# Experts' rows turned by VectorE and regrouped through DRAM instead of transposed by TensorE

## Chip, cores and metric

The kernel runs on one core of a Trainium2 chip. The metric is the time of one execution on the device in microseconds (us); lower is better. Fast and slow differ here by fractions of a per cent: the three runs of the kernel before lie between 3649.78 and 3657.06 us.

## What is computed

Three layers, one after the other, on 8 sequences of 3072 tokens with 256 channels (24576 tokens), all in float32:

```python
def _attn_ref(x, filt_r, filt_i):            # a filter in the frequency domain
    Y = np.fft.rfft(x, axis=1) * (filt_r + 1j * filt_i)[None]
    return np.fft.irfft(Y, n=x.shape[1], axis=1)

def _moe_ref(x, w_gate, w_output_gate, w1, w2):   # 8 experts, each token to one
    e_idx = np.argmax(x @ w_gate, axis=1)
    for e in range(E):
        mask = e_idx == e
        h = np.maximum(x[mask] @ w1[e], 0.0)
        out[mask] = gate_w[mask, None] * eom[mask, e, None] * (h @ w2[e])

def _moe2_ref(x, w_in, w_out):               # a layer for all tokens
    h = x @ w_in
    return (h / (1.0 + np.exp(-1.702 * h))) @ w_out
```

## The kernel before

The program has three stages. The first (to about 540 us) filters the sequences by a Fourier transform in steps and leaves the rows of all tokens in DRAM (`yn`), and a table that lists each expert's tokens (`xid`). The second, about 540 to 1690 us, runs the experts. The third, to the end, runs the last layer and puts each row in its token's place. The change lies in the second stage alone.

**Blocks and slots.** `experts(js)` runs over a list `js` of blocks, one expert each: 41 full blocks of 512 rows and 17 halves of 256 (four more halves stand behind a branch that isn't taken here). The first 11 are full; from then on every third is a half. A block has eight slots (`f` from 0 to 7). In each slot TensorE runs `gemm1` of this slot (six matmuls, L590) and `gemm2` of the slot two before (six matmuls, L599). Every operand is split in a high and a low part, so that three products give float32 accuracy. ScalarE makes the high part `hh` with the rectifier (L912) and VectorE the low part `hl` (L913); `gemm2` two slots later uses both. In the same slot an eighth of the next block's weights is split (`split_w`, L654 on ScalarE, L655 on VectorE). While full blocks run, VectorE also converts the last layer's weights, a piece a slot (`convert`, L745 to L759), from about 700 to 1130 us.

**How rows come in.** For block `j` of the list, the next `ja` and the one after it `jb`:

- `load_tok(jb)` in slot 4 (POOL): an indirect DMA loads the tokens' numbers (`ids` L667, for halves `it` L688), then four indirect DMAs (two for a half) gather 128 rows of 256 each into `xg` (L693). Two buffers of `xg`.
- `scale_x(ja)` in slot 2 (POOL): the rows of `xg` are multiplied by their gate (L705).
- `prep_x(ja, k)` at the end of slots 4 and 5: `split_t` has TensorE transpose `xg` (L575, four for a full block, two for a half) into PSUM, and `split_out` makes `xh` (ScalarE, L580) and `xl` (VectorE, L581) from it.
- `load_w(jb, 0)` and `load_w(jb, 1)` in slots 3 and 7 (SP's queue): the weights, 1 MB each, into one buffer each (`w1r` L618, `w2r` L623). SP also stores a block's results (`zt`, L949) in slot 1 of the block after it.

Each engine runs its instructions in the order in which the program writes them and stands where one has to wait. POOL isn't bound to the slots as such: it runs ahead as far as buffers allow. Only while tokens are still being scattered into `xid` (`scatter`, L399 and L402, one each slot, in blocks 0 to 6) does each of its steps wait for a tick of that slot. `NE` is the number of first blocks that take tokens of the first four sequences alone, so that they needn't wait for the last scatters.

`turn_rows` in the third stage has VectorE turn 32x32 blocks (L1168, `V.transpose`), and lets 16 DMAs put these in place. The experts' stage doesn't use it before the change.

Of the kernel before, what the change touches and what calls it, by code (L numbers as in the profile page):

```python
# [24 lines left out]
NT = 32  # L25
CAP = NTOK
NFULL = 41
NE = 8
BE = 4
NX = 5  # L30
NU = 5
# [95 lines left out]
def fftconv_moe_moe2(ctx: ExitStack, tc: tile.TileContext, x, ffl, fny, wg, w1, w2, win, wout,  # L127
# [5 lines left out]
    yn = tc.dram_tile([NTOK, D], F32, name="yn")  # L133
    zt = tc.dram_tile([2, 128, NZ], F32, name="zt")
    idc = tc.dram_tile([NZ - ZREM, 1], I32, name="idc")
    us = [tc.dram_tile([N1, N2, D], F32, name=f"us{b}") for b in range(NB)]

    keep = ctx.enter_context(tc.tile_pool(name="keep", bufs=1))
# [436 lines left out]
            T.transpose(p[:, c, :], xg[:, c, 128 * k:128 * k + 128], eye)  # L575
        return p

    def split_out(p, nt, xh, xl, k):
        w = slice(0, 128 * nt)
        S.copy(xh[:, k, w], p[:, 0:nt, :].rearrange("p c t -> p (c t)"))  # L580
        V.tensor_tensor(xl[:, k, w], p[:, 0:nt, :].rearrange("p c t -> p (c t)"),  # L581
                        xh[:, k, w].bitcast(F32), op=ALU.subtract)

    def gemm1(wh, wl, xh, xl, f, w):
        p = pools["ph"].tile([128, 512], F32, name="ph", tag="ph")
# [86 lines left out]
    def load_tok(j):  # L672
        if j is None:
            return
        nt = nt_of(j)
        assert j < NE or not (scat or gating)
        if nt == 4:
            if j in named:
                G.memset(gap, 0.0)
            else:  # L680
                load_ids(j)
            it = ids[:, j]
        else:
            G.memset(gap, 0.0)
            it = pools["m"].tile([128, 2, 2], I32, name="it")
            for c in range(2):
                o = NFULL + 2 * (j - NFULL) + c
                G.indirect_dma_start(  # L688
                    out=it[:, c, :], out_offset=None, in_=xid,
                    in_offset=bass.IndirectOffsetOnAxis(ap=xidx[:, o:o + 1].bitcast(U32), axis=0))  # L690
        t = pools["m"].tile([128, 4, D], F32, name="xg")
        for c in range(nt):
            i = G.indirect_dma_start(  # L693
                out=t[:, c, :], out_offset=None, in_=yn if j >= NE else yn[0:BE * SEQ, :],
                in_offset=bass.IndirectOffsetOnAxis(ap=it[:, c, 0:1].bitcast(U32), axis=0))
            early(j, i)
        xg[j] = t, it
# [13 lines left out]

    rof = {}

    def prep_x(j, k):
        if j is None:
            return
        if k == 0:
            xt[j] = [pools["xt"].tile([128, 2, 512], F32R, name="xh"), pools["xt"].tile([128, 2, 512], F32R, name="xl")]
        p = split_t(xg[j], nt_of(j), k)
        split_out(p, nt_of(j), *xt[j], k)  # L720
        if k == 1:
            xg.pop(j)

    cv = {}

# [96 lines left out]
    for k in range(ng * NB + 4 + nu):  # L822
        b, i = divmod(k, ng)
        if k == kt:
            c1.close()
            c1p.close()
            open_expert_pools()
            load_tok(0)
        if k < kt:
            load_u(k + NU - 1)  # L830
            if k < 6:
                load_f(k + 2)
            prep_f(k + 2)
            if k == 8:
                nc.sync.dma_start(smt, t_sm)
            swap(k - 1)
            filt_a(k)
            filt_b(k - 1)
            inv2_out(k - 3)
            if k in s1_at:  # L840
                stage1(s1_at[k])
                stage1_out(s1_at[k])
            inv2(k - 2)
        if k in t2_at:
            trans(*t2_at[k])
        if k - 1 in t2_at:
            inv1(*t2_at[k - 1])
        if kt <= k < kt + 7:
            for m in PARTS[max(0, k - kt + 1 if k > kt else 0):k - kt + 2]:
                load_part(0, m)  # L850
        if kt + 4 < k < kt + 9:
            for m in PARTS[2 * (k - kt - 5):2 * (k - kt - 5) + 2]:
                split_w(0, m)
        if k == kt + 9:
            load_w(1, 0)
        if k == kt + 11:
            load_w(1, 1)
        if k == kt + 3:
            scale_x(0)
        if k == kt + 6:  # L860
            load_tok(1)
        if k in (kt + 9, kt + 10):
            prep_x(0, k - kt - 9)
        if k in (kt - 24, kt - 22):
            load_ids((k - kt + 24) // 2)
        if 3 <= k < kt:
            pb, pg = divmod(k - 3, ng)
            scatter(2, gts[pb % 2][:, 0, 0, 8 * pg:8 * pg + 1])
        elif k in t2_at:
            scatter(1, tick(gq[t2_at[k]][:, 0, 0:1]))  # L870
        go_on(2 if k < kt else 1)
        if i == 1 and b > 1:
            go_on(1000)
            gating.append(gate(b - 2, psa, "pt"))
            if b - 2 == BE - 1:
                gating.append(early_tables())
# [9 lines left out]
        nc.sync.dma_start(zg[j], zt[:, :, at].rearrange("k p n -> p k n"))  # L886

    first = {}

    def experts(js):  # L890
        ex = None
        hq, pz = {}, {}
        ns = 8 * len(js)
        js = js + [None, None]
        for t in range(ns + 2):
            if t == ns - 12 and not first:
                first["rest"] = nc.values_load(eidx[0:1, NBLK:NBLK + 1], min_val=0, max_val=NREM)
                tc.mark_branch_hint_location("rest", "LikelyTaken", [ET.PE, ET.DVE, ET.Activation])
            if t == ns - 8 and "hi" not in first:
                first["hi"] = pools["z0"].tile([128, 2, 512], F32R, name="z0h", bufs=1)  # L900
                for k in range(2):
                    z, h = zg[0][:, k, :], first["hi"][:, k, :]
                    S.copy(h, z)
                    V.tensor_tensor(z.bitcast(F32R), z, h.bitcast(F32), op=ALU.subtract)
            n, f = divmod(t, 8)
            j, ja, jb = (js + [None])[n:n + 3]
            if t < ns:
                w = 128 * nt_of(j)
                p = gemm1(wt[j][0], wt[j][1], *xt[j], f, w)
                hh = pools["m"].tile([128, 512], F32R, name="hh", bufs=3)  # L910
                hl = pools["m"].tile([128, 512], F32R, name="hl", bufs=3)
                S.activation(hh[:, 0:w], p[:, 0:w], AF.Relu)  # L912
                V.scalar_tensor_tensor(hl[:, 0:w], p[:, 0:w], 0.0, hh[:, 0:w].bitcast(F32),  # L913
                                       op0=ALU.max, op1=ALU.subtract)
                hq[t] = hh, hl
                split_w(ja, f)
                if f == 3:
                    load_w(jb, 0)
                if f == 7:
                    load_w(jb, 1)  # L920
                if f == 4:
                    load_tok(jb)
                scatter(1, tick(hh[:, 0:1].bitcast(F32)))
                go_on(1)
                if f == 2:
                    scale_x(ja)
                if not wm and not gating and not scat:
                    open_layer_pools()
                    S.activation(gap2, gap2, AF.Gelu_apprx_sigmoid)
                    ex = extra()  # L930
                if ex is not None and j < NFULL and next(ex, 0) == 0:
                    cvs.close()
                    ex = None
                    pools["z0"] = ctx.enter_context(tc.tile_pool(name="z0p", bufs=1, side="right", reuse_waits="tile"))
                    load_z(0, pools["z0"])
            if t >= 2:
                j2, f2 = js[(t - 2) // 8], (t - 2) % 8
                nt = nt_of(j2)
                w2 = 128 * nt
                if f2 == 0:  # L940
                    pz[j2] = pz_tiles(nt)
                hh, hl = hq.pop(t - 2)
                gemm2(hh, hl, wt[j2][2], wt[j2][3], f2, pz[j2], w2)
                if f2 == 7:
                    zo = pools["m"].tile([128, 2, 512], F32, name="zo")
                    for k, z in enumerate(pz.pop(j2)):
                        S.copy(zo[:, k, 0:w2], z)
                    at = slice(512 * j2, 512 * j2 + 512) if nt == 4 else bass.ds(rof.pop(j2) + ZREM, 256)
                    nc.sync.dma_start(zt[:, :, at].rearrange("k p n -> p k n"), zo[:, :, 0:w2])  # L949
                    wt.pop(j2)  # L950
                    xt.pop(j2)
            if t < ns and f in (4, 5):
                prep_x(ja, f - 4)

    order = list(range(NFULL))
    for n, j in enumerate(range(NFULL, NALW)):
# [2 lines left out]
    with tc.If(first["rest"] > NALW - NFULL, label="rest"):  # L959
        for j in (NALW, NALW + 1):  # L960
            load_w(j, 0)
            load_w(j, 1)
            load_tok(j)
            if j == NALW:
                for i in range(8):
                    split_w(j, i)
        scale_x(NALW)
        prep_x(NALW, 0)
        prep_x(NALW, 1)
        experts(list(range(NALW, NBLK)))  # L970
    c2.close()
    nc.sync.dma_start(idr, idc[0:NTOK - ZREM, :].rearrange("(m p) o -> p (m o)", p=128))
# [443 lines left out]
```

## Time and profile before

| | |
|---|---|
| median of three runs | 3650.39 us (3649.78 to 3657.06) |
| the profiled execution | 3652.92 us, of this the span of its instructions 3651.2 us |
| mean granted TensorE clock | 0.996 |
| busy: TensorE, VectorE, ScalarE, POOL | 98%, 71%, 70%, 60% of the span |

The profile gives for each engine its instructions with start and duration. Matmuls overlap, so a matmul's duration is longer than its share of time; what it costs is read from the distance between the starts of two of them. "Idle before" is the time in which the engine stood ahead of the instruction, with what ended it behind the arrow.

### The profile page before, as it was taken

To read this page: it belongs to the slowest core of one execution; us is meant where nothing else is said; L and a number is where in the kernel's file an instruction comes from. 1 tells how busy PE (TensorE), PEld (TensorE's weight loads), DVE (VectorE), ACT (ScalarE), POOL (GpSimd) and SP (SyncE) were. 2 spreads that over 40 slices of the span, in tenths; PEclk is the share of its full clock that TensorE was granted. 3 is DMA by queue.
4 is the path that set the end of the run, shared out by engine and by line. 5 is a ranking of instruction groups with operands and counts; after the bars stand their busy time and mean duration, and the time that the engine had idled before them with its cause. 6 is when DMAs were issued, how large, how long until landed. Compare 5 with 4: busy or idle time off the path is not lost.

```text
span 3651.2 us, 69267 instructions
## 1 busy us (share of the span) xinstructions
PE 3594.6 (98%) x24924; PEld 3298.0 (90%) x24924; DVE 2586.2 (71%) x4738; ACT 2569.9 (70%) x4954; POOL 2184.2 (60%) x2313
## 2 busy tenths in 40 slices
PE   6999999999999999999999999999999999999998
PEld 4777777888888888889999999999999999999998
DVE  5667768688887656565777777776777777777776
ACT  4777784555555555555788888887888888888886
POOL 3044466633333333333677877777777777877776
PEclk8999999999999999999999999999999999999999
DMA  9666644455665555552112111211121111111111
GB/s 278 208 204 198 186 143 144 156 173 153 191 174 165 159 143 170 148 153 64 33 40 44 42 39 38 48 36 39 38 48 36 39 39 47 36 39 41 46 36 33
DMA packets 422077, 369.34 MB, mean 101 GB/s; under 512 B 239265, under 2 KB 328737, under 8 KB 421729
## 3 DMA queue, kind: packets, MB, share of 16 engines
q1 hardware_dynamic: 394016, 313.28, 31.6%
q0 software_dynamic: 27296, 51.56, 4.6%
q8 instruction: 198, 3.24, 0.4%
q14 instruction: 151, 1.23, 0.1%
q10 hardware_dynamic: 416, 0.03, 0.0%
HBM read 238.43 MB, written 101.66 MB: 93 GB/s over the span
## 4 chain that ended last, share of the span: by engine, by line
PE 42%; POOL 4%; ACT 2%; SPq 2%; issue 2%; DVE 1%; DMA 0%; POOLq 0%; DVEq 0%; ACTq 0%
PE ph L1002 21%; PE pz L1145 20%; SPq L1173 2%; POOL hl L1104 2%; ACT hh L1100 1%; POOL xl L1023 1%; PE pz L1002 1%; ACT ph L1087 1%; POOL zg L1042 0%; ACT xh L1014 0%; POOL out_dram L1074 0%; ACT sp L1083 0%; POOL zg L1041 0%; DMA zo<-ev 0%; DVE hl L1104 0%
## 5 line engine op out<-in xcount | busy, mean ns | idle before, releaser
L1104 POOL TENSOR_TENSOR hl<-q,hh 128x512 fp32r<-128x512 f32 x734 | 931.9, 1295 | 292.2 <-ACT hh L1100 290.3
L912 ACT ACTIVATE hh<-ph 128x512 fp32r<-128x512 f32 (+1 forms) x464 | 248.3, 535 | 476.5 <-PE ph L590 467.2
L913 DVE SCALAR_TENSOR_TENSOR hl<-ph,hh 128x512 fp32r<-128x512 f32 (+1 forms) x464 | 283.3, 610 | 280.0 <-ACT hh L912 279.0
L1100 ACT CAST hh<-q 128x512 fp32r<-128x512 f32 x740 | 464.0, 627 | 18.2 <-DVE q L1342 15.3
L1002 PE MATMUL ph<-xh,winh 128*128 128x256 f32 x1504 | 425.0, 283 | 0.7 <-DVE ph L1192 0.7
L1002 PE MATMUL ph<-xh,winl 128*128 128x256 f32 x1504 | 424.0, 282 | 0.0
L693 POOL DMA_INDIRECT xg<-yn,ids x164 | 171.8, 1048 | 417.8 <-PE ph L575 357.2
L1002 PE MATMUL ph<-xl,winh 128*128 128x256 f32 x1504 | 421.7, 280 | 0.0
L1087 ACT ACTIVATE ph<-ph 128x512 f32<-128x512 f32 x580 | 339.9, 586 | 91.1 <-DVE ph L1192 79.7
L1145 PE MATMUL pz<-hh,woutl 128*128 128x256 f32 x1472 | 380.8, 281 | 0.0
L1145 PE MATMUL pz<-hh,wouth 128*128 128x256 f32 x1472 | 377.9, 280 | 0.0
L1192 DVE TENSOR_TENSOR ph<-ph,sp 128x512 f32<-128x512 f32 x376 | 262.4, 698 | 145.3 <-PE ph L1002 145.3
L1192 DVE TENSOR_TENSOR q<-ph,sp 128x512 f32<-128x512 f32 x188 | 128.2, 682 | 332.1 <-PE ph L1002 331.8
L1104 DVE TENSOR_TENSOR hl<-ph,hh 128x512 fp32r<-128x512 f32 x486 | 331.7, 682 | 26.3 <-ACT hh L1100 25.3
L1083 ACT COPY sp<-ph 128x512 f32<-128x512 f32 x564 | 332.3, 589 | 22.7 <-PE ph L1002 19.6
L590 PE MATMUL ph<-xh,w1h 128*128 128x512 f32 (+1 forms) x928 | 343.9, 371 | 0.0
L590 PE MATMUL ph<-xh,w1l 128*128 128x512 f32 (+1 forms) x928 | 333.6, 359 | 0.0
L590 PE MATMUL ph<-xl,w1h 128*128 128x512 f32 (+1 forms) x928 | 333.4, 359 | 0.0
L599 PE MATMUL pz<-hh,w2h 128*128 128x512 f32 (+1 forms) x928 | 333.3, 359 | 0.0
L599 PE MATMUL pz<-hl,w2h 128*128 128x512 f32 (+1 forms) x928 | 332.8, 359 | 0.0
L599 PE MATMUL pz<-hh,w2l 128*128 128x512 f32 (+1 forms) x928 | 332.7, 359 | 0.0
L1002 PE MATMUL ph<-xh,sh 128*128 128x256 f32 x1128 | 322.3, 286 | 7.2 <-ACT sp L1083 6.6
(273 smaller groups left out, 11355.2 us busy)
## 6 DMA issues: line engine op xcount, KB each, us to landing
w1r<-in_w_dram SPq DMA_DIRECT2D x57, 1024.0 KB, 4.9
w2r<-in_w_dram SPq DMA_DIRECT2D x57, 1024.0 KB, 5.8
u<-us SPq DMA_DIRECT2D x128, 192.0 KB, 3.5
zg<-zt SPq DMA_DIRECT2D x48, 512.0 KB, 3.7
zo<-ev SPq DMA_DIRECT2D x752, 32.0 KB, 2.0
yn<-yt SPq DMA_DIRECT2D x90, 256.0 KB, 2.8
xt<-in_x_dram SPq DMA_DIRECT2D x84, 256.0 KB, 3.4
us<-u SPq DMA_DIRECT2D x84, 256.0 KB, 2.6
```

The source lines that it names most:

```text
L590: T.matmul(p[:, 0:w], a[:, k, ws], b[:, k, 0:w], start=n == 0, stop=n == 5)
L599: T.matmul(z[k], a[:, f, ks], b[:, 0:w], start=f == 0 and n == 0 and (w == 512 or k == 0), stop=n == 2, skip_group_check=True)
L693: i = G.indirect_dma_start(out=t[:, c, :], out_offset=None, in_=yn if j >= NE else yn[0:BE * SEQ, :], in_offset=bass.IndirectOffsetOnAxis( ...
L912: S.activation(hh[:, 0:w], p[:, 0:w], AF.Relu)
L913: V.scalar_tensor_tensor(hl[:, 0:w], p[:, 0:w], 0.0, hh[:, 0:w].bitcast(F32), op0=ALU.max, op1=ALU.subtract)
L1002: T.matmul(out, a[u], b[v], start=start and n == 0, stop=stop and n == 2, skip_group_check=True)
L1083: S.copy(snaps[n], x)
L1087: S.activation(t, src, AF.Gelu_apprx_sigmoid)
L1100: S.copy(hq[s, n][0], t)
L1104: eng.tensor_tensor(l, t, h.bitcast(F32), op=ALU.subtract)
L1145: T.matmul(o, w[k][u], x[v][:, k, :], start=start, stop=n == 5, skip_group_check=True)
L1192: V.tensor_tensor(o, a, b, op=ALU.add)
```

## The change

After it, blocks 0 and 1 of the list are transposed by TensorE as before. From block 2 on a block's rows take another way, laid down in the table `PLAN` (one list for each of the first three blocks of the run, one for all others; an entry is slot, step, and how many blocks ahead):

- `gather` three blocks ahead in slot 2 and `scale` in slot 6; `xg` has one buffer instead of two.
- `turn` two blocks ahead in slot 1: one VectorE instruction turns the 32x32 blocks of `xg` into a `zo` tile, and SP stores it (512 KB) to a DRAM buffer `xs`, of which there are two.
- `fetch` two blocks ahead in slot 4: four DMAs of SP load it back as `xq`, regrouped so that all channels of a half stand on 128 partitions. Two buffers.
- `prep0` and `prep1` for the next block in slots 4 and 5: `split_out` as before, but from `xq` in SBUF.

`NE` grows from 8 to 10, and block 1's gather moves behind block 0's transposes.

```diff
-NE = 8
+NE = 10
...
-    def split_out(p, nt, xh, xl, k):
-        w = slice(0, 128 * nt)
-        S.copy(xh[:, k, w], p[:, 0:nt, :].rearrange("p c t -> p (c t)"))
-        V.tensor_tensor(xl[:, k, w], p[:, 0:nt, :].rearrange("p c t -> p (c t)"),
-                        xh[:, k, w].bitcast(F32), op=ALU.subtract)
+    def split_out(src, nt, xh, xl, k):
+        h, l = (t[:, k, 0:128 * nt].rearrange("p (c a f) -> p c a f", a=4, f=32) for t in (xh, xl))
+        S.copy(h, src)
+        V.tensor_tensor(l, src, h.bitcast(F32), op=ALU.subtract)
...
-        t = pools["m"].tile([128, 4, D], F32, name="xg")
+        t = pools["m"].tile([128, 4, D], F32, name="xg", bufs=1)
...
+    def turn_x(j):
...
+        nt = nt_of(j)
+        n = 64 * nt
+        t = pools["m"].tile([128, 2, 512], F32, name="zo").rearrange("p k n -> p (k n)")[:, 0:4 * n]
+        V.transpose(t.rearrange("p (b g f) -> p g b f", b=4, f=32),
+                    xg.pop(j)[:, 0:nt, :].rearrange("p c (k b f) -> p (c k) b f", k=2, f=32))
+        nc.sync.dma_start(xs[j % 2][:, 0:4 * n], t)
+
+    def fetch_x(j):
...
+        n = 64 * nt_of(j)
+        turned[j] = pools["xt"].tile([128, 1024], F32, name="xq")
+        for a in range(4):
+            nc.sync.dma_start(turned[j][:, n * a:n * a + n],
+                              xs[j % 2][32 * a:32 * a + 32, 0:4 * n].rearrange("i (b e) -> b i e", b=4))
...
-        p = split_t(xg[j], nt_of(j), k)
-        split_out(p, nt_of(j), *xt[j], k)
-        if k == 1:
-            xg.pop(j)
+        if j in xg:
+            src = split_t(xg[j], nt, k)[:, 0:nt, :].rearrange("p c (a f) -> p c a f", f=32)
+            if k == 1:
+                xg.pop(j)
+        else:
+            src = turned[j][:, 0:256 * nt].rearrange("p (a c k f) -> p k c a f", a=4, k=2, f=32)[:, k]
+            if k == 1:
+                turned.pop(j)
+        split_out(src, nt, *xt[j], k)
...
-        if k == kt + 6:
-            load_tok(1)
         if k in (kt + 9, kt + 10):
             prep_x(0, k - kt - 9)
+        if k == kt + 10:
+            load_tok(1)
...
+    OPS = {"gather": load_tok, "scale": scale_x, "turn": turn_x, "fetch": fetch_x,
+           "prep0": lambda j: prep_x(j, 0), "prep1": lambda j: prep_x(j, 1)}
+    PLAN = (((2, "scale", 1), (4, "prep0", 1), (5, "prep1", 1), (6, "gather", 2)),
+            ((0, "scale", 1), (1, "turn", 1), (1, "gather", 2), (3, "fetch", 1), (4, "scale", 2),
+             (6, "turn", 2), (6, "prep0", 1), (7, "prep1", 1), (6, "gather", 3)),
+            ((0, "fetch", 1), (1, "scale", 2), (3, "turn", 2), (3, "gather", 3), (4, "prep0", 1), (5, "prep1", 1),
+             (5, "fetch", 2), (6, "scale", 3)),
+            ((1, "turn", 2), (2, "gather", 3), (4, "fetch", 2), (4, "prep0", 1), (5, "prep1", 1), (6, "scale", 3)))
...
                 split_w(ja, f)
+                run("turn")
                 if f == 3:
                     load_w(jb, 0)
                 if f == 7:
                     load_w(jb, 1)
-                if f == 4:
-                    load_tok(jb)
+                run("fetch", "gather")
                 scatter(1, tick(hh[:, 0:1].bitcast(F32)))
                 go_on(1)
-                if f == 2:
-                    scale_x(ja)
+                run("scale")
...
-            if t < ns and f in (4, 5):
-                prep_x(ja, f - 4)
+            if t < ns:
+                run("prep0", "prep1")
```

In the order in which the instructions stand, three places move. The first is POOL in blocks 1 and 2 (`xg` are gathered rows, `ids` the tokens' numbers; a pair of `gap` and `xid` is one scatter, and further pairs are left out at "..."). Before, the scaling of block 2, the gather of block 3 and its scaling:

```order
L705 TENSOR_TENSOR xg_5618<-xg_5618,ids_75 128x1024
L399 COPY gap_120<-ticks_74 128x1
L402 DMA xid_57<-tid_5139,pos_5515 196608x2
L666 MEMSET gap_120 128x1
L667 DMA ids_75<-xid_57,xidx_79 128x8
L693 DMA xg_5862<-yn_58,ids_75 128x256 x4
...
L705 TENSOR_TENSOR xg_5862<-xg_5862,ids_75 128x1024
```

After, the scalings of blocks 2, 3 and 4, each but the first with its gather:

```order
L705 TENSOR_TENSOR xg_5683<-xg_5683,ids_77 128x1024
...
L693 DMA xg_5775<-yn_58,ids_77 128x256 x4
...
L705 TENSOR_TENSOR xg_5775<-xg_5775,ids_77 128x1024
L400 COPY gap_122<-ticks_76 128x1
L403 DMA xid_57<-tid_5141,pos_5517 196608x2
L666 MEMSET gap_122 128x1
L667 DMA ids_77<-xid_57,xidx_81 128x8
L693 DMA xg_5931<-yn_58,ids_77 128x256 x4
...
L705 TENSOR_TENSOR xg_5931<-xg_5931,ids_77 128x1024
```

Before, eight scatters stood between one scaling and the next; after, four stand between the scalings of 2 and 3 and five between those of 3 and 4, so that POOL gathers and scales two blocks in about one.

The second place is VectorE in slots 1 and 2 of a full block that converts weights (`cvt` and `cvm` belong to the conversion). After:

```order
L952 SCALAR_TENSOR_TENSOR hl_7959<-ph_7951,hh_7958 128x512
L655 TENSOR_TENSOR w1l_7935<-w1r_7804,w1h_7934 128x512
L723 STREAM_TRANSPOSE zo_7964<-xg_7761 128x8x4x32
L952 SCALAR_TENSOR_TENSOR hl_7987<-ph_7979,hh_7986 128x512
L655 TENSOR_TENSOR w1l_7935<-w1r_7804,w1h_7934 128x512
L774 TENSOR_SCALAR cvt_7999<-cvr_7861 128x256
```

Before, the next slot's `hl` followed the split directly; now the turn of a later block's rows stands between them.

The third place is SP in one full block. Before:

```order
L949 DMA zt_59<-zo_7256 128x2x512
...
L618 DMA w1r_7312<-in_w1_dram 128x2x1024
L739 DMA cvr_7376<-in_win_dram 128x512
...
L623 DMA w2r_7431<-in_w2_dram 128x8x256
L739 DMA cvr_7483<-in_win_dram 128x512
```

After:

```order
L725 DMA xs0_61<-zo_7488 128x1024
L768 DMA cvr_7491<-in_win_dram 128x512
L987 DMA zt_59<-zo_7499 128x2x512
...
L618 DMA w1r_7561<-in_w1_dram 128x2x1024
L734 DMA xq_7585<-xs0_61 128x1x256 x4
L768 DMA cvr_7618<-in_win_dram 128x512
...
L623 DMA w2r_7679<-in_w2_dram 128x8x256
```

The store of the turned rows comes ahead of the results' store, and the four loads stand between the two weights.

## Rows read from the trace of the kernel before

**Rows 1.** Windows: stretch, length, busy of PE, PEld, DVE, ACT, POOL, PEclk, DMA, GB/s.
```profile
557.00:697.00 140.00, 136.72 (x620) 112.35 (x619) 99.33 (x215) 71.23 (x169) 102.90 (x136) 0.99 0.43 140
726.44:749.15 22.71, 22.71 (x105) 18.80 (x104) 22.02 (x48) 11.00 (x20) 8.88 (x9) 1.00 0.51 164
848.88:906.38 57.50, 57.50 (x309) 49.53 (x308) 49.44 (x107) 30.52 (x60) 21.00 (x20) 1.00 0.63 173
1136.38:1193.88 57.50, 57.50 (x309) 49.53 (x308) 34.45 (x55) 30.64 (x60) 19.95 (x20) 1.00 0.60 156
```

**Rows 2.** Timeline of TensorE: start, duration, then the instruction.
```profile
558.25 0.60 PE L575 MATMUL ph<-sq,xg 128*128 128x128 f32 x4
561.45 0.60 PE L575 MATMUL ph<-sq,xg 128*128 128x128 f32 x4
...
723.23 0.60 PE L575 MATMUL ph<-sq,xg 128*128 128x128 f32 x4
...
1113.43 0.39 PE L599 MATMUL pz<-hl,w2h 128*128 128x512 f32 x1
1113.66 0.60 PE L575 MATMUL ph<-sq,xg 128*128 128x128 f32 x4
1114.02 0.48 PE L590 MATMUL ph<-xh,w1h 128*128 128x512 f32 x1
1114.33 0.40 PE L590 MATMUL ph<-xl,w1h 128*128 128x512 f32 x1
...
1116.88 0.60 PE L575 MATMUL ph<-sq,xg 128*128 128x128 f32 x4
```

**Rows 3.** Instructions of line 575: count, duration in ns (least, median, most), first and last start.
```profile
L575 PE MATMUL ph<-sq,xg x396: 270/272/332, 539.7 to 1672.8; 128*128 128x128 f32 x198
```

**Rows 4.** POOL's groups from 557 to 697: busy us, mean ns, idle before.
```profile
L402 POOL DMA_INDIRECT xid<-tid,pos x47 | 48.1, 1024 | 8.6 <-issue 6.4 <-ACT ticks L417 1.4 <-ACT hh L912 0.5
L693 POOL DMA_INDIRECT xg<-yn,ids x24 | 24.7, 1030 | 26.2 <-issue 13.4 <-DMA ids<-xid,xidx 5.5 <-PE ph L590 3.7
L399 POOL COPY gap<-ticks 128x1 f32<-128x1 f32 x47 | 13.2, 280 | 1.1 <-ACT ticks L417 0.9
L705 POOL TENSOR_TENSOR xg<-xg,ids 128x1024 f32<-128x1024 f32 x6 | 11.4, 1906 | 0.2
L667 POOL DMA_INDIRECT ids<-xid,xidx x6 | 6.2, 1036 | 1.1 <-issue 1.1
```

**Rows 5.** Timeline of POOL in block 0, and of TensorE in block 3.
```profile
552.96 0.18 POOL L399 COPY gap<-ticks 128x1 f32<-128x1 f32 x1 [8.00 <-ACT ticks L417]
...
554.81 1.92 POOL L705 TENSOR_TENSOR xg<-xg,ids 128x1024 f32<-128x1024 f32 x1
...
626.89 0.39 PE L599 MATMUL pz<-hl,w2h 128*128 128x512 f32 x1
629.72 0.71 PE L575 MATMUL ph<-sq,xg 128*128 128x128 f32 x4 [2.44 <-POOL xg L705]
...
634.57 0.60 PE L575 MATMUL ph<-sq,xg 128*128 128x128 f32 x4
```

**Rows 6.** Instructions of line 1168, the layer's turn.
```profile
L1168 DVE STREAM_TRANSPOSE ev<-ev x47: 1245/1246/1248, 1744.9 to 3608.2; 128x1024 f32<-128x1024 f32 x47
```

**Rows 7.** Timeline of TensorE and VectorE: a slot's start, its hl, hl's use.
```profile
1108.22 0.39 PE L590 MATMUL ph<-xh,w1h 128*128 128x512 f32 x1
...
1110.49 0.68 DVE L913 SCALAR_TENSOR_TENSOR hl<-ph,hh 128x512 fp32r<-128x512 f32 x1
...
1115.95 0.40 PE L599 MATMUL pz<-hl,w2h 128*128 128x512 f32 x1
```

**Rows 8.** DMA issues from 540 to 1690: count, size of each, median us to landing.
```profile
w1r<-in_w_dram SPq DMA_DIRECT2D x57, 1024.0 KB, 4.9
...
zt<-zo SPq DMA_DIRECT2D x41, 512.0 KB, 3.2
```

**Rows 9.** Timeline of SP and ScalarE in a half block and behind it.
```profile
980.77 0.38 SPq L618 DMA_DIRECT2D w1r<-in_w_dram  x1
...
988.35 0.61 ACT L654 CAST w1h<-w1r 128x512 fp32r<-128x512 f32 x1
```

More of the change, by code (lines that the diff above doesn't have):

```diff
@@ L135, in fftconv_moe_moe2 @@
     idc = tc.dram_tile([NZ - ZREM, 1], I32, name="idc")
+    xs = [tc.dram_tile([128, 1024], F32, name=f"xs{i}") for i in range(2)]
     us = [tc.dram_tile([N1, N2, D], F32, name=f"us{b}") for b in range(NB)]
@@ L712, in fftconv_moe_moe2 @@
     rof = {}
+    turned = {}
+    def turn_x(j):
+        if j is None:
+            return
+        nt = nt_of(j)
[5 more added lines that the diff above has]
+    def fetch_x(j):
+        if j is None:
+            return
+        n = 64 * nt_of(j)
[3 more added lines that the diff above has]
+                              xs[j % 2][32 * a:32 * a + 32, 0:4 * n].rearrange("i (b e) -> b i e", b=4))
     def prep_x(j, k):
@@ L716, in prep_x @@
             return
+        nt = nt_of(j)
         if k == 0:
             xt[j] = [pools["xt"].tile([128, 2, 512], F32R, name="xh"), pools["xt"].tile([128, 2, 512], F32R, name="xl")]
-        p = split_t(xg[j], nt_of(j), k)
-        split_out(p, nt_of(j), *xt[j], k)
-        if k == 1:
-            xg.pop(j)
+        if j in xg:
[7 more added lines that the diff above has]
+        split_out(src, nt, *xt[j], k)
     cv = {}
@@ L906, in experts @@
             j, ja, jb = (js + [None])[n:n + 3]
+            events = [(op, (js + [None] * 4)[n + m]) for at, op, m in PLAN[min(n, 3)] if at == f]
+            run = lambda *names: [OPS[op](m) for op, m in events if op in names]
             if t < ns:
@@ L962, in fftconv_moe_moe2 @@
             load_w(j, 1)
-            load_tok(j)
             if j == NALW:
+                load_tok(j)
                 for i in range(8):
@@ L969, in fftconv_moe_moe2 @@
         prep_x(NALW, 1)
+        load_tok(NALW + 1)
         experts(list(range(NALW, NBLK)))
```

## The prediction, made before the changed kernel had run

> **What bounds the kernel now.** I read the windows of the experts' stretch first, then TensorE's timeline there, then POOL's groups and its timeline in the first seven blocks, then VectorE's and the DMA rows. The windows [rows 1] show TensorE busy without a gap from the eighth block on: 57.50 us of 57.50 for a run of two blocks of 512 rows and one of 256, and the same 57.50 both in the stretch where VectorE also converts the layer's weights (busy 49.44 us) and in the one after it (34.45). VectorE's load moves by 15 us and the period doesn't move at all, so TensorE alone sets it. The window of one full block lasts 22.71 us; its borders, like the others', are starts of transposes. The first seven blocks are different. From the fifth slot of block 0 to that of block 7 the transposes' starts lie 558.25 to 723.23 apart [rows 2], 164.98 us, where seven periods of 22.71 would be 159.0: 6.0 us are lost, and POOL is why. Its groups from 557 to 697 [rows 4], busy and idle together, fill the whole 140 us, and TensorE stands before a transpose until POOL's scaling ends [rows 5].
>
> **What the change removes.** Four transposes cost TensorE this: the matmul before them starts at 1113.43, the second one behind them at 1114.33 [rows 2], 0.90 us for what takes two spacings of about 0.227 (1113.43 to 1113.66) without them. That is 0.446 us for four, 0.112 each; their busy time of 273 ns each [rows 3] overlaps and is not the price. 396 stand in the trace [rows 3]; blocks 0 and 1 keep theirs (16), 380 go. Of these 48 lie in blocks 1 to 6 (for blocks 2 to 7), 5.4 us, and 332 behind, 33 full blocks by 8 and 17 halves by 4: **37.2 us** on a path that has no gap. A full block is then 21.82 us, a slot (an eighth) 2.73.
>
> **What it adds.** VectorE turns each block once. The nearest row is the layer's turn of 128x1024 [rows 6], 1.25 us; that one is in place and this one writes pieces of 32, so I bound it by 1.25 and 2.5 (every element paid twice) and take 1.25, the same operation on the same size. ScalarE and VectorE split from SBUF instead of PSUM with the same shapes: I cost that at nothing, hidden beside TensorE, since ScalarE is busy 30.5 of 57.5 us [rows 1]. SP gets one store and four loads a block, five issues at about 0.4 us [rows 9], beside the few weights, results and conversion pieces that it issues in a block. Behind the store, which waits for VectorE, stand the store of the results and the next weights; behind the loads, which wait for the store to land (a store of 512 KB lands in 3.2 us [rows 8]), only the second weights. Stored in slot 1 and loaded in slot 4, 8 us later, the rows are needed a block after that: hidden.
>
> **Where VectorE is the cover.** It issues in order, so a late turn holds up the next hl. How much it may be late: hl of the slot that starts at 1108.22 is done at 1110.49 + 0.68 = 1111.17 and is first used at 1115.95 [rows 7], and 0.45 us of that are transposes, so 4.3 us. In the blocks with conversion and no halves between them (five of them, blocks 6 to 10) VectorE is busy 22.02 us of 22.71 [rows 1], with the turn 23.3 against 21.82: at worst 5 x 1.45 = 7 us, less the 4.3 of slack. Later the halves let it catch up (49.44 + 2 x 1.25 + 0.65 = 52.6 against 57.50 less 20 transposes = 55.26). Bounds 0 and 7, I take **+3**, the worst case less the slack.
>
> **The first seven blocks** are the uncertain term. By [rows 4] a scatter costs POOL (48.1 + 8.6 + 13.2)/47 = 1.49 us, the ids and four gathers (24.7 + 26.2 + 6.2 + 1.1)/6 = 9.7, a scaling 1.9: with eight scatters 23.5 us a block, more than TensorE's 21.82. The change asks POOL for one block more in the same time: block 1 gathers blocks 3 and 4 and scales 2 and 3. And the single xg buffer makes each gather wait for the turn before it. POOL's order gives the chain. Scaling 1 starts at 554.81 [rows 5] as before. Gather 2 can begin when block 1's rows have left xg, 561.45 + 0.60 [rows 2]; with 9.7 for the gather, three scatters and the scaling, scaling 2 ends at 578.1. VectorE reaches that turn in slot 1 of block 1. Block 0 began five slots ahead of 558.25, at 544.6, so block 1 begins at 567.3 (21.82 and its own eight transposes in block 0), and the turn is due 6.3 us into it (a slot, 2.95 to the end of hl [rows 7], 0.6 for the split), 573.6: 4.5 late, 0.2 more than the slack. Scaling 3 ends 9.7 + 4 x 1.49 + 1.9 = 17.6 later at 595.7, its turn is due in slot 6 at 587.5: 8.2 late, 4.0 beyond the slack. Scaling 4 (one scatter more) ends at 614.8 and is due at 605.1: 5.4 beyond. Scaling 5 at 633.9, due at 626.9: 2.7. Then POOL sets the pace with 23.6 against 21.8 until the scatters end in block 6: three times 1.8. Together 17.7 us. After a stand of 2.6 us (626.89 to 629.72 less a spacing) TensorE ran its next matmuls at about half the rate: the transposes at 629.72 and 634.57 lie 4.85 apart, elsewhere 3.22 (1113.66 to 1116.88) [rows 2, 5]; that is 1.6 us again for each long stand, which I count for the two longest, 3.2. Against before: the 6.0 lost there go, the 5.4 of 48 transposes go, 17.7 + 3.2 come: **+9.5**. Bounds: -11.4, if POOL's lag is always covered; +15.4, if no slack covers (4.3 more) and the third stand pays the clock too. I take the chain, since it uses POOL's own rows.
>
> **Sum:** -37.2 + 9.5 + 3 = -24.7. The profiled execution took 3652.92 (span 3651.2, the rest around it) and would be 3628.2; it lies 2.5 above the median of the three runs, 3650.39, so I predict **3626 us**.
>
> **A rule against it.** The rows show a transpose on TensorE at 0.112 us, eight of them 0.9, and the turn on VectorE at 1.25 [rows 2, 6]. The Trainium skill, "VectorE: DVE Perf Modes", sections "The three transpose paths" and "Rules for kernel authors", says that VectorE only turns 32x32 blocks within themselves and that for 128x128 TensorE is to be used if the result may go to PSUM. By that rule the step should have stayed. No row makes VectorE's time the block's time past the conversion, so the sum stands; what the rule would mean is the second rival.
>
> **Rivals.**
> 1. POOL's lead is enough. Then the first seven blocks give 11.4 us instead of costing 9.5: 3650.4 - 37.2 - 11.4 + 3 = 3605. For it: POOL stands idle for 8.0 us at the start of block 0 [rows 5]. Against it: that idle time waits for a tick, and afterwards 140 us of 140 are filled. Chance 0.18.
> 2. VectorE becomes the bound (slower than before). If each turn's 1.25 us (0.65 for a half) falls on hl's path, 33 x 1.25 + 17 x 0.65 = 52.3 us come for the 37.2 that go, and with the first blocks' 15.4 that is 3650.4 + 15.1 + 15.4 = 3681. It decides from where VectorE's need exceeds TensorE's block: 21.82 us. For it: 22.02 in a converting block. Against it: 34.45 of 57.50 afterwards. This is also where the skill's rule would be right. Chance 0.04.
> 3. Weights land late. The regrouping moves 1 MB more in a full block, on top of 156 to 173 GB/s [rows 1]. In a half block the next first weights are issued at 980.77 and used at 988.35, 7.6 us [rows 9], and land in 4.9 [rows 8]. With 4.3 us of slack behind that, TensorE pays only from about 11.5 us on; to eat the 24.7 us, 17 halves would have to pay 1.5 us each (no change, 3650), with 2 us each 3659. Chance 0.06 for no change, 0.05 for slower.
> The forecast itself has 0.67.
>
> **How the numbers follow.** The forecast's own terms span 3602 (first bound -11.4, conversion 0) to 3636; rival 1 lies inside, and a part of rival 3 and of the doubled turn (1.25 us more in each of 39 full blocks would cost only where VectorE is tight, some 6 us) stretches the top to 3642. What is left out is below 2 in 10. No change means within 0.2%, 7.3 us, about what a measurement can tell: 0.06. Faster 0.85, slower 0.09.
>
> **What would show it.** Right: periods of 55.3 us for two full blocks and a half all through, no transposes after block 0, VectorE's turns at 1.25 us, waits of the turn on POOL's scaling in blocks 1 to 6 only, block 7 about 10 us later than before. Wrong: a period that stays near 57.5 (rival 2 or 3, told apart by what the hl or the weights' split waits for), or blocks 1 to 6 at 21.8 us (rival 1).

## The result, and the profile after

The changed kernel is **slower**: 3686.94 us (3679.73 to 3691.56) beside 3653.24 (3649.78 to 3657.06) for the kernel before on the same chip, a ratio of 1.0092 with a 95% interval from 1.008 to 1.0103. The profiled execution took 3685.92 us. The forecast was 3626 us and a range that ended at 3642: wrong in sign, 61 us too low (58 when both are taken beside the kernel before on their chip).

The windows cut the experts' stretch in a part with POOL's scatters, a part with the conversion and the rest (stretch, length, then busy time of PE, PEld, DVE, ACT and POOL, PEclk, DMA share, GB/s). Before:

```profile
540.00:740.00 200.00, 196.16 (x892) 160.45 (x891) 152.84 (x333) 102.23 (x231) 134.70 (x167) 0.99 0.47 153
740.00:1240.00 500.00, 500.00 (x2649) 429.36 (x2649) 405.03 (x831) 263.10 (x515) 172.94 (x171) 1.00 0.60 169
1240.00:1700.00 460.00, 459.02 (x2537) 398.79 (x2537) 273.02 (x432) 244.50 (x487) 151.30 (x153) 1.00 0.55 148
```

After:

```profile
540.00:740.00 200.00, 180.14 (x769) 144.15 (x768) 136.01 (x309) 93.93 (x217) 129.83 (x161) 0.96 0.55 174
740.00:1240.00 500.00, 473.75 (x2328) 397.35 (x2327) 416.82 (x850) 243.98 (x486) 160.37 (x163) 0.97 0.71 207
1240.00:1700.00 460.00, 452.38 (x2345) 387.01 (x2344) 294.82 (x464) 243.28 (x489) 149.92 (x153) 1.00 0.73 201
```

TensorE, which stood for 3.8 us of the first 200 before, now stands for 19.9. From 740 on, where it had stood for 1.0 us in all, it now stands for 26.3 and 7.6, and in the conversion's part the granted clock is 0.97 in place of 1.00. What it waits for there stands in the waits of 740 to 1700 (engine, line, what it waited for: us in all, times, longest):

```profile
ACT w2h L654 <- DMA w2r<-in_w_dram: 114.5, 24, 9.9
DVE w2l L655 <- ACT w2h L654: 96.6, 21, 8.4
PEld pz L599 <- ACT hh L951: 24.2, 10, 4.5
PE pz L599 <- ACT hh L951: 19.9, 10, 4.1
ACT w1h L654 <- DMA w1r<-in_w_dram: 17.9, 11, 3.2
PE pz L599 <- DVE hl L952: 13.7, 15, 2.1
```

ScalarE stands before the split of the **second** weights for a transfer that hasn't landed, VectorE behind it, and because both issue in order, `hh` and `hl` of the running slot are late for TensorE. The kernel before has no wait for `w2r` in this list. One such place, SP's timeline after:

```profile
884.33 0.33 SPq L725 DMA_DIRECT2D xs<-zo  x1
884.76 0.39 SPq L987 DMA_DIRECT2D zt<-zo  x1
886.83 0.41 SPq L618 DMA_DIRECT2D w1r<-in_w_dram  x1
887.68 3.98 SPq L734 DMA_DIRECT2D xq<-xs  x4
893.05 0.69 SPq L710 DMA_DIRECT2D idc<-it  x1
893.94 0.51 SPq L623 DMA_DIRECT2D w2r<-in_w_dram  x1
```

ScalarE's and TensorE's timelines behind it:

```profile
909.75 0.62 ACT L654 CAST w2h<-w2r 128x512 fp32r<-128x512 f32 x1 [8.36 <-DMA w2r<-in_w_dram]
```
```profile
908.52 0.39 PE L590 MATMUL ph<-xh,w1l 128*128 128x512 f32 x1
911.43 0.50 PE L599 MATMUL pz<-hh,w2h 128*128 128x512 f32 x1 [2.52 <-ACT hh L951]
911.77 0.40 PE L599 MATMUL pz<-hh,w2l 128*128 128x512 f32 x1
914.20 0.80 PE L599 MATMUL pz<-hl,w2h 128*128 128x512 f32 x1 [2.04 <-DVE hl L952]
```

And windows of 2 us:

```profile
890.00:892.00 2.00, 2.00 (x13) 1.76 (x12) 1.33 (x4) 0.60 (x1) 0.00 (x0) 1.00 0.97 391
...
898.00:900.00 2.00, 2.00 (x11) 1.65 (x10) 2.00 (x5) 1.11 (x2) 0.00 (x0) 1.00 1.07 46
900.00:902.00 2.00, 2.00 (x11) 1.65 (x10) 1.90 (x6) 0.60 (x1) 0.00 (x0) 1.00 0.50 24
902.00:904.00 2.00, 2.00 (x11) 1.65 (x10) 1.93 (x6) 0.00 (x0) 0.00 (x0) 1.00 0.51 30
...
906.00:908.00 2.00, 2.00 (x10) 1.66 (x9) 0.00 (x0) 0.00 (x0) 0.00 (x0) 1.00 1.04 349
...
914.00:916.00 2.00, 1.80 (x4) 1.49 (x5) 2.00 (x5) 0.42 (x1) 0.00 (x0) 0.50 0.87 173
```

`w2r` is issued at 893.94 and first used at 909.75, 15.8 us later; ScalarE was ready for it 8.36 us earlier, at 901.4, so the room was 7.5 us. For 4 us the DMA engines are half busy and move 24 and 30 GB/s, and then 349. What was issued 0.9 us ahead of `w2r` is line 710, the **list** of 256 token numbers of a later half block: 1 KB as 256 pieces of 4 bytes. TensorE stands for 2.52 and 2.04 us and runs at a granted clock of 0.50 behind it (the lower of its two levels, 1.2 GHz); in the window from 920 to 926 it is back at 1.00.

The same trace holds the comparison. From 740 to 1700, 17 loads of `w2r` follow a list on the queue: they are used 11.1 to 18.0 us after their issue, every one is waited for, and they make 106.4 of the 114.5 us. The other 31 are used after 5.4 to 11.7 us, with 8.1 us of waits in all.

Line 710 is part of `scale_x`. Before, the scaling sat in slot 2 of the block ahead of the half, and the list went out ahead of the first weights: at 900.38, the weights at 904.45, and these were wanted only at 916.26. The change moves `scale` to slot 6, and the list with it, directly ahead of slot 7's second weights. I had counted the step's POOL work, and not the DMA that it issues on SP's queue.

### The profile page after: what moved, and what is told of

Its sections match the earlier page's. It is cut to its first block, busy times and chain, and to the rows that moved or that the text cites. A ratio compares the mean times of both kernels' runs of the same rounds, so it can differ in the third digit from the quotient of the medians.

```text
span 3684.1 us, 69251 instructions
## 1 busy us (share of the span) xinstructions
PE 3577.9 (97%) x24544; PEld 3270.9 (89%) x24544; DVE 2624.3 (71%) x4794; ACT 2560.4 (69%) x4954; POOL 2178.0 (59%) x2313
## 4 chain that ended last, share of the span: by engine, by line
PE 39%; POOL 5%; SPq 3%; ACT 3%; issue 2%; DVE 1%; DMA 0%; POOLq 0%; DVEq 0%; ACTq 0%
PE ph L1041 20%; PE pz L1184 19%; SPq L1212 3%; POOL hl L1143 2%; ACT hh L1139 1%; POOL xl L1062 1%; PE pz L1041 1%; ACT ph L1126 1%; POOL out_dram L1113 1%; POOL zg L1081 0%; ACT xh L1053 0%; DMA zo<-ev 0%; ACT sp L1122 0%; POOL zg L1080 0%; DVE q L1231 0%
## 5 line engine op out<-in xcount | busy, mean ns | idle before, releaser
L693 POOL DMA_INDIRECT xg<-yn,ids x164 | 162.7, 992 | 332.4 <-DMA ids<-xid,xidx 163.7
L599 PE MATMUL pz<-hh,w2h 128*128 128x512 f32 (+1 forms) x928 | 337.3, 363 | 19.9 <-ACT hh L951 19.9
```

The costliest lines, as they stand in the source:

```text
L599: T.matmul(z[k], a[:, f, ks], b[:, 0:w], start=f == 0 and n == 0 and (w == 512 or k == 0), stop=n == 2, skip_group_check=True)
L693: i = G.indirect_dma_start(out=t[:, c, :], out_offset=None, in_=yn if j >= NE else yn[0:BE * SEQ, :], in_offset=bass.IndirectOffsetOnAxis( ...
```

## Experiments

Theory A: the list's small pieces hold up the second weights. Theory B (the prediction's third rival): the 1 MB more per block does. Ratios are to the kernel before on the same chip; they are what to compare, since its median was between 3652.45 and 3666.05 us from chip to chip.

**List back in its old place.** `list_x` is split out of `scale_x` and runs in slot 2 of the block ahead.

```diff
-            off = nc.sync.value_load(rofs[0:1, j - NFULL:j - NFULL + 1], min_val=0, max_val=NTOK - ZREM)
-            rof[j] = off
-            nc.sync.dma_start(idc[bass.ds(off, 256), :].rearrange("(c p) o -> p c o", p=128), it[:, :, 0:1])
+            listed[j] = it
...
+    LIST = (2, "list", 1)
```

> The changed kernel, with one step moved: the 1 KB store of a half block's token numbers (idc, 256 pieces of 4 bytes) goes out in slot 2 of the block ahead of that half, where it stood before the change, instead of in slot 6 of the half three blocks ahead of it, right before that block's second weights. The regrouping through DRAM stays. Theory A (the list's small pieces hold up the second weights, which land after 15 us): the waits for w2r behind halves go, some 35 us of TensorE's stands after 740 us with the slow clock behind them, 3687 to about 3647. Theory B (the added 1 MB a block makes the weights late): about the same as the changed kernel, 3680 to 3690.

3704.55 us, 1.0143 (1.0126 to 1.016): worse than the changed kernel, which neither theory had. Now both weights are late, in 740 to 1700 `w1r` for 49.9 us (22 times) and `w2r` for 79.3 (21 times). In this traffic the old place of the list is no better than the new one.

**Only the list, in the kernel before.** Slot 6 of the half, ahead of `w2r`, nothing else changed.

```diff
+                if f == 6:
+                    list_x(j)
```

> The kernel before, with the same step alone moved: the list of a half goes out in slot 6 of that half itself, right ahead of the second weights, instead of in slot 2 of the block ahead. Nothing goes through DRAM in addition. Theory A: the second weights land about 15 us after their issue where 10.6 and 4.3 us of slack are there, so 17 halves pay a few us each, 3653 to about 3670 to 3690. Theory B: no difference, 3653.

3662.26 us, 1.0032 (1.002 to 1.0043). This lies between the two forecasts. The loads of `w2r` behind a list are used 10.6 to 12.3 us after their issue, and no wait for `w2r` is over 1.5 us (7.0 us in all). By the ratio the place alone costs some 12 us; the profiled execution, the fastest of the seven (3655.47 us), shows only a part of it.

**No round trip.** The turn writes straight into `xq`; no store, no reloads. The rows are then not regrouped.

```diff
-        t = pools["m"].tile([128, 2, 512], F32, name="zo").rearrange("p k n -> p (k n)")[:, 0:4 * n]
+        turned[j] = pools["xt"].tile([128, 1024], F32, name="xq")
+        t = turned[j][:, 0:4 * n]
...
-        nc.sync.dma_start(xs[j % 2][:, 0:4 * n], t)
```

> The changed kernel without the round trip: VectorE turns the 32x32 blocks right into the tile that the split reads, so no store to DRAM and no loads back (the rows aren't regrouped, so the product is of other rows). The list stays in slot 6 ahead of the second weights. Theory A: the late second weights stay; only the first blocks' waits for the reloaded rows and for the first conversion piece go, 3687 to about 3672. Theory B: the weights are in time, some 40 us go besides, about 3635.

3636.21 us, 0.9954 (0.9937 to 0.997): B's number. But the list is still in its pieces and still ahead of `w2r`, and behind it `w2r` still takes 8.9 to 15.8 us to its use, with 28.1 us of waits. So this run and the one before it contradict a theory of either alone.

**New way from block 8 on.** Blocks 2 to 7 are transposed by TensorE again; the list is in its old place.

```diff
+    LEAD = 6
...
+        lead = LEAD if len(js) > 8 else 0
...
-            events = [(op, (js + [None] * 4)[n + m]) for at, op, m in PLAN[min(n, 3)] if at == f]
+            events = [(op, (js + [None] * 4)[n + m]) for at, op, m in PLAN[max(0, min(n - lead, 3))] + (LIST,) if at == f]
```

> Experiment e1 with the start moved: blocks 0 to 7 are transposed by TensorE with the first list of the plan, and the new way begins with block 8, when the scatters are done and POOL is free. Theory A and my chain for POOL in the first blocks: the first stretch costs as before the change, 324 transposes of 0.112 us (36 us) go, and a few us come in the converting blocks: about 3620. Theory B: the late weights stay, about 3660.

3689.8 us, 1.0101 (1.0084 to 1.0118), 15 us better than the first run, and above both forecasts: most of the early stands go (7.5 us from 540 to 740 in place of 19.7), the late ones stay.

**Packed list, four transfers.** VectorE turns the list into eight rows of 32 numbers.

```diff
+            V.tensor_copy(col[:, :, 0:1], it[:, :, 0:1])
+            V.transpose(rowl, col.rearrange("p c f -> p (c f)"))
+            for b in range(4):
+                nc.sync.dma_start(idc[bass.ds(off, 256), :].rearrange("(c b i) o -> b o c i", b=4, i=32)[b],
+                                  rowl[32 * b:32 * b + 1, :].rearrange("o (c i) -> o c i", c=2))
```

> The changed kernel with one edit: the half block's list of 256 numbers is turned by VectorE into eight rows of 32 numbers and stored by four transfers of 256 bytes in place of 256 pieces of 4 bytes. Place in the program, bytes of the rows' round trip and all else as in the changed kernel. Theory A (the list's small pieces hold up the queue in front of the second weights): the waits for w2r (114.5 us on ScalarE in the changed kernel) fall below 30 us, the late stretch's stands (some 43 us) mostly go, 3645 to 3655 us. Theory B (the 1 MB more per block fills the transfers, whatever stands between): at most 10 us better, 3677 to 3687 us.

> As the packed list, and the new way only from the eighth block on (the first seven blocks behind block 0 are turned by TensorE as before). Theory A: the early stands (some 24 us) go too and some 6 us of transposes come back, 3625 to 3637 us. Theory B: 3662 to 3672 us.

3710.77 us, 1.0118 (1.0096 to 1.014), and 3707.34, 1.0113 (1.0096 to 1.013). Both lie above every range that was forecast. They are no test of A, as SP's waits in the first of the two show (740 to 1700):

```profile
SPq L719 <- DMA idc<-rowl: 98.2, 38, 6.6
```

Each of the four stores waits for the one before to land. SP is held for some 10 us a list, and `w2r` behind it is issued late instead of landing late (ScalarE's wait for it is 109.1 us).

**Regrouping inside SBUF.** 16 transfers of 32 partitions from `zo` to `xq`, no DRAM.

> The changed kernel without the way through DRAM: the turned rows are regrouped by 16 transfers from SBUF to SBUF, so half the bytes (512 KB in place of 1 MB per full block) and no store that a load must wait for; the list stays in its 256 pieces in front of the second weights. Theory A: the waits for w2r stay above 80 us, 3670 to 3690 us. Theory B: half of what leaving the round trip out gave, 3655 to 3665 us.

> All three together: new way from the eighth block, packed list, regrouping from SBUF to SBUF. Theory A: as the second of these runs, 3620 to 3635 us, the regrouping worth little beside the packed list. Theory B: 3630 to 3645 us, at least 25 us below the second of these runs. Either way it should be below the kernel before.

3852.84 us, 1.0513 (1.0495 to 1.053), and 3824.99, 1.0425 (1.0408 to 1.0442): far off, and for a reason of its own. SP in the first:

```profile
915.80 11.03 SPq L728 DMA_DIRECT2D xq<-zo  x16
926.93 0.53 SPq L985 DMA_DIRECT2D zt<-zo  x1
928.30 0.40 SPq L618 DMA_DIRECT2D w1r<-in_w_dram  x1
```

Sixteen issues take 11 us a block, 0.69 each, and `w1r` behind them goes out late (302 us of ScalarE's waits from 540 to 1700). Half the bytes, but sixteen issues in place of five. ScalarE's waits for `w2r` are 17.8 us there, where A expected over 80; in a kernel 5% slower this is no clean test of either theory.

**Packed list, one transfer.** The same turn, then one transfer of eight rows of 128 bytes.

```diff
+            nc.sync.dma_start(idc[bass.ds(off, 256), :].rearrange("(c b i) o -> b c (i o)", b=4, i=32),
+                              rowl[0:128:32, :].rearrange("b (c i) -> b c i", c=2))
```

> The packed list again, its eight rows of 128 bytes in one transfer: in the run with four, each of the four waited for the one before to land (98 us of waits on SP's queue, 10.3 us per half block), so that run put one delay in the place of another. Theory A (small pieces): the waits for w2r fall from 114.5 to under 30 us and the late stands go, 3645 to 3660 us (some 24 us of early stands stay). Theory B (bytes): 3677 to 3687 us.

3637.81 us, **0.9954** (0.9937 to 0.9971), even below A's range. Windows, then the waits of 740 to 1700, then SP's timeline:

```profile
740.00:1240.00 500.00, 497.47 (x2539) 423.87 (x2538) 442.24 (x909) 267.40 (x530) 174.23 (x178) 1.00 0.70 222
1240.00:1700.00 460.00, 459.70 (x2537) 402.12 (x2536) 298.10 (x493) 252.83 (x508) 157.77 (x169) 1.00 0.59 189
```
```profile
ACT w2h L659 <- DMA w2r<-in_w_dram: 17.4, 15, 2.1
```
```profile
881.23 2.41 SPq L743 DMA_DIRECT2D xq<-xs  x4
885.00 1.44 SPq L718 DMA_DIRECT2D idc<-rowl  x1
886.65 0.40 SPq L628 DMA_DIRECT2D w2r<-in_w_dram  x1
```

The same bytes, the same order, the list in the same place: the waits for `w2r` fall from 114.5 to 17.4 us, the issue at 886.65 is used at 895.43, 8.8 us later in place of 15.8, and TensorE is busy again at full clock, while the DMA engines move more per us than in the changed kernel (222 beside 207 GB/s from 740 to 1240). This is A, and it settles that the bytes alone are not what makes the weights late.

**With the late start.** Packed list in one transfer, new way from block 8 on.

> The packed list in one transfer, and the new way only from the eighth block on. Theory A: 3622 to 3637 us. Theory B: 3655 to 3670 us.

3625.68 us, **0.9923** (0.9906 to 0.9939): faster than both kernels.

**Round trip on another queue.** Store and reloads issued by POOL.

```diff
-        nc.sync.dma_start(xs[j % 2][:, 0:4 * n], t)
+        G.dma_start(xs[j % 2][:, 0:4 * n], t)
```

> The changed kernel with the round trip's store and four reloads issued from GpSimd's queue in place of SP's, at the same places of the program; the bytes are the same, the list stays in 256 pieces on SP's queue. Theory B (bytes on the transfer engines): 3675 to 3700 us, second weights as late as in the changed kernel. Theory C (SP's queue is served in order: its waits for the turn, some 300 us, and for the store, 63 us, and what lies in the queue ahead of the weights are the cost): the waits for w2r fall below 50 us, 3640 to 3665 us, unless GpSimd's own issues make its chain late.

3810.97 us, 1.0439 (1.042 to 1.0458). The time is no answer about the queue: POOL now stands for the turn before it stores, its next gather and scaling come late, and the turn waits for them. Waits from 540 to 1700:

```profile
DVE zo L723 <- POOL xg L705: 217.3, 26, 14.9
POOL xs L725 <- DVE zo L723: 155.4, 37, 9.9
PEld pz L599 <- DVE hl L952: 140.5, 36, 12.3
```

The waits for `w2r` do answer a part: they are 98.1 us, 86.0 of them at the 14 loads behind a list (9.9 to 15.7 us from issue to use), though the round trip is no longer on their queue. So its place on SP's queue is not what makes them late there, against theory C. That its bytes on the DMA engines are is what is left; it is argued, not shown by a run of its own.

The Trainium skill, "Perfetto Trace Analysis", section "DMA Optimizations", says that spreading transfers over the engines that can issue them may help where making the descriptors is the bottleneck. No row of the changed kernel shows that condition to hold. The move cost 3.5 points more than staying on SP (1.0439 against 1.0092).

**Packed list in the kernel before.**

> The kernel before with the list packed into eight rows of 128 bytes and stored in one transfer at the list's old place. In the kernel before, w1r behind the list is used without a wait, so all theories expect no change: within 5 us of the kernel before. It measures how long w1r takes behind a packed list (some 5 us in place of 11).

3650.84 us, 0.9997 (0.9988 to 1.0007): nothing to win there. The queue's row gives an estimate of what the pieces cost all the same (packets, MB, share of 16 engines' span), of the kernel before, of this one, and of the run above with only the list moved:

```profile
q1 hardware_dynamic: 394016, 313.28, 31.6%
```
```profile
q1 hardware_dynamic: 389596, 313.28, 29.4%
```
```profile
q1 hardware_dynamic: 394016, 313.28, 30.2%
```

2.2% of 16 engines' 3652 us are 1290 us for 17 lists, 76 each: 0.3 us for each piece of 4 bytes. But the third row has the packets of the first at 30.2%, and from it the difference is 0.8%, or 0.1 us a piece. So the estimate is 0.1 to 0.3. How long a list takes to land is measured directly, in the kernel before (count, size, median us to landing):

```profile
idc<-it SPq DMA_DIRECT2D x17, 1.0 KB, 9.5
```

**Neither, and a still later start.**

> Neither: the turned rows stay where VectorE puts them (no store, no reload; the rows are not regrouped, so the products are those of other rows) and the list goes out packed in one transfer. It closes the square of four: both in (the changed kernel), only the list in small pieces (3636 us), only the round trip (3638 us), neither. If each were a cost of its own, leaving out both would give the sum, some 100 us below the changed kernel: 3587 us. If it takes both together to make the second weights late, little is left to win: 3622 to 3634 us.

> The packed list in one transfer and the new way from three blocks later than in the run from the eighth block, when GpSimd no longer gates the last batch: the stand of 5 us at its first block and some 2 us behind it should go, and three more blocks of transposes cost 3 times some 1 us: 3619 to 3627 us, no more than 6 us below that run, and within 3 us of it if the stand comes with the start of the new way wherever that lies.

3627.11 us, 0.9907 (0.9891 to 0.9924), and 3630.2 us, 0.991 (0.9894 to 0.9927). The first closes the square of four, as ratios:

| | list in 256 pieces | list packed |
|---|---|---|
| with the round trip | 1.0092 | 0.9954 |
| without | 0.9954 | 0.9907 |

From the changed kernel either step alone gives 1.38 points, 50 us; once the other is done it gives 0.47, 17 us (each ratio is known to about 0.2 points). The run with neither was on a chip where the kernel before took 3662.39 us; by the medians as they stand the second step gives only 9 to 11 us. So each has a small cost of its own, and two thirds or more of what either gives back needs both: the round trip's traffic (207 GB/s in all), and a stop in SP's queue just ahead of weights with 7.5 us of room. The second run can't be told in time from the start at block 8 (0.9923). The stands of 4.93 and 1.14 us at the first new block there became three of 0.73, 0.72 and 1.90 here, so about half of them goes. That POOL no longer scatters by then is the likely reason, and is not shown by itself; what it gives is about what three more blocks of transposes cost.

## Why the prediction was wrong, step by step

- **The step that failed** is in "What it adds": "behind the loads, which wait for the store to land ..., only the second weights ... hidden". Ahead of the second weights that go out in a half block also stands the list, which the change moves there with `scale`, and which I did not name at all. The runs show in its place: 15.8 us from issue to use where 7.5 were to be had, and 8.8 with the list packed. Naming the move would not have been enough: with the list back in its old place the kernel was slower still (1.0143). The step also put at nothing what the round trip's traffic does to whatever lies behind the list.
- **The third rival** had the right effect, weights that land late, but one of its two causes and the wrong transfer. It looked at the first weights (room 7.6 us, [rows 9]), set TensorE's threshold at about 11.5 us with the slack (7.6 and 4.3 add up to 11.9), and found 4.9 us of landing [rows 8]. For the second weights the room was 7.5, 11.8 with the slack; 15.8 less that are 4.0 us, and TensorE stood for 2.52 + 2.04 = 4.56 at that place. The threshold held there, at the one place read; its chance of 0.05 for slower came from costing every transfer at an undisturbed landing time.
- **The late stretch** accounts for most of the miss. From the changed kernel to the packed list TensorE's stands from 740 to 1700 fall by 33.9 - 2.8 = 31.1 us, and the clock's 0.97 over 500 us is worth some 15 (an estimate from the rounded row): together 46 us, where the two profiled executions are 45.8 apart (spans of 3684.1 and 3638.3).
- **The transposes** were priced rightly. Where nothing is late, two full blocks and a half take 55.10 us (predicted 55.3), here in the run with neither cost:

```profile
1300.80:1355.90 55.10, 55.10 (x290) 47.51 (x289) 37.66 (x59) 30.10 (x60) 19.81 (x20) 1.00 0.48 163
```

- **The turn**, taken at the lower bound of 1.25 to 2.5 us, takes 1.25 us for a full block, though it writes pieces of 32. Second rival: VectorE's rise from 34.45 to 37.66 us in that period didn't move it. The Trainium skill, "VectorE: DVE Perf Modes", section "The three transpose paths", says that VectorE turns only blocks of 32x32. The kernel agrees in that its turned rows have to be regrouped. Leaving the regrouping out, with the list packed, is worth 0.47 points (11 us by the medians as they stand).
- **The first seven blocks** were right in kind and short in size. POOL's scalings and VectorE's turns, after:

```profile
577.18 1.89 POOL L705 TENSOR_TENSOR xg<-xg,ids 128x1024 f32<-128x1024 f32 x1 [0.80 <-DMA xg<-yn,ids]
593.69 1.90 POOL L705 TENSOR_TENSOR xg<-xg,ids 128x1024 f32<-128x1024 f32 x1
611.86 1.91 POOL L705 TENSOR_TENSOR xg<-xg,ids 128x1024 f32<-128x1024 f32 x1
630.93 1.91 POOL L705 TENSOR_TENSOR xg<-xg,ids 128x1024 f32<-128x1024 f32 x1
```
```profile
579.10 1.25 DVE L723 STREAM_TRANSPOSE zo<-xg 128x1024 f32<-128x1024 f32 x1 [4.21 <-POOL gap L666]
595.63 1.25 DVE L723 STREAM_TRANSPOSE zo<-xg 128x1024 f32<-128x1024 f32 x1 [6.90 <-POOL xg L705]
614.24 1.23 DVE L723 STREAM_TRANSPOSE zo<-xg 128x1024 f32<-128x1024 f32 x1
633.31 1.23 DVE L723 STREAM_TRANSPOSE zo<-xg 128x1024 f32<-128x1024 f32 x1
```

  The scalings were predicted to end at 578.1, 595.7, 614.8 and 633.9, and end at 579.1, 595.6, 613.8 and 632.8: POOL's chain is right to about a microsecond, so the first rival falls. ScalarE's first split of weights in block 7 comes at 728.9 and the one in block 0 at 548.8; before, these stood at 711.7 and 549.7. That is 18 us more where 9.5 were predicted. In the run with neither cost it is 13; the other 5 are the round trip's.

  What the chain made of the late turns was wrong in its parts. TensorE's two longest stands there are these:

```profile
596.43 0.80 PE L590 MATMUL ph<-xh,w1h 128*128 128x512 f32 x1 [5.59 <-ACT xh L581]
718.82 0.79 PE L599 MATMUL pz<-hl,w2h 128*128 128x512 f32 x1 [6.51 <-DVE hl L952]
```

  It stood for nothing at the turn at 614, where 5.4 us were predicted, and for 2.95, 2.42 and 6.51 us at 683, 709 and 719, where three times 1.8 were. Ahead of the stand at 596 ScalarE waits for reloaded rows (7.8 us), but in the run with neither cost TensorE stands for 6.72 us at the same place, so the round trip's 5 us are not there. They lie in the last three stands: 11.9 us here, 6.0 in that run. At 719 VectorE waits for the first piece to convert, which SP issues behind a late store.
- **Conversion, +3**: with the packed list TensorE stands for 2.5 us in all of 740 to 1240, and in the run with neither cost for none. The bounds of 0 and 7 hold; the 3 us themselves are not confirmed.
- **The sum**, -24.7 us or a ratio of 0.9932, is what the kernel gives when the late weights are gone and the start lies behind most of the scatters (0.9923), by other terms: it pays for six more blocks of transposes and not for the early stands. That the two numbers agree is luck.

## What to carry to other kernels

When a step is moved, list every instruction that it issues, and for each DMA what stands behind it on its queue and how much room that has. A small transfer is costed by its pieces and not by its bytes alone, and its price is paid by what is queued behind it. Test two suspected causes in all four combinations, because a delay can be hidden under each alone and not under both.

## What the runs showed of the hardware

- A store of 1 KB in pieces of 4 bytes cost an estimated 0.1 to 0.3 us of a DMA engine per piece and landed in 9.5 us in the kernel before, and in the changed kernel's traffic a load of 1 MB behind it took 15.8 us from issue to use; as eight rows of 128 bytes, 8.8 us. The Trainium skill, "DMA: Bandwidth & Descriptors", section "Specifications", wants 512 bytes and more for a transfer at full rate; the runs agree in direction, and rows of 128 bytes were enough here.
- SP's issue isn't free: 0.4 us for one transfer alone, 0.69 each for sixteen in a row, and up to 6.27 us for one `cvr` load after the changed kernel's list, at 899.25.
- Behind the stands of 2.52 and 2.04 us TensorE ran at a granted clock of 0.50, from 914 to 920; over the conversion's part the lower clock cost some 15 us (an estimate: 3% of 500 us) beside 26.3 us of stands.
- With the round trip on POOL's queue, `w2r` behind a list was nearly as late as on SP's (9.9 to 15.7 us from issue to use beside 11.1 to 18.0): another queue did not keep this traffic out of its way.
